# Cutting the two last weight loads of a decode kernel into pieces for unequally late DMA engines

## The chip, the cores and the metric

The kernel runs on one core of one Trainium2 chip. The metric is device time in microseconds (us), the median of several executions. The six executions of the kernel before lie within 0.62 us of each other, and the whole argument is about one microsecond in 1267. So the clean evidence is in the traces; the times only have to agree with it.

## The reference, cut to what matters

One decode step: attention of 16 query heads over 8 cached K/V heads of 65,536 positions and 256 dimensions, then the output projection `wo`; a small MLP beside it is cut here.

```python
q = (x @ wq).reshape(B, Sq, 16, 256).transpose(0, 2, 1, 3)
k = jnp.repeat(k_cache, 2, axis=1)      # k_cache, v_cache: 1 x 8 x 65536 x 256, bf16
v = jnp.repeat(v_cache, 2, axis=1)
p = softmax(einsum("bhqd,bhkd->bhqk", q, k) * 256 ** -0.5)
o = einsum("bhqk,bhkd->bhqd", p, v)
a = o.transpose(0, 2, 1, 3).reshape(B, Sq, 4096) @ wo     # wo: 4096 x 448
# ... MLP branch b and gate g cut ...
return g * a + (1 - g) * b
```

Reading the two caches once is 537 MB of the 544.22 MB that the kernel reads, at 430 GB/s over its 1264.3 us, and that is the kernel's time.

## The kernel before: the parts that matter

One queue (SP) issues all large loads: 32 K loads and 32 V loads of 8 MB, with the `wo` rows of a head pair between them. The last V load is cut into pieces along the sequence, so that the work behind each piece can start early. The `wo` rows of the last two query heads come last of all.

```python
pieces = [(NFIRST, NLATE), (NLATE, 124), (124, NV)]      # 96:112, 112:124, 124:128
# ... sync engine, last K/V block ...
load(vbuf, A_v_cache, j, 0, NFIRST if last else NV, 0, sem_v)
if last:
    for (n0, n1), sem in zip(pieces, sem_vp):
        load(vbuf, A_v_cache, j, n0, n1, 0, sem)
# ... cut ...
eng.wait_ge(s_proj, H - 1)
for h in range(REP):                                     # REP = 2
    w = A_wo[(HQ - REP + h) * DH:(HQ - REP + h + 1) * DH, :]
    eng.dma_start(wo_sb[:, h, :], w.rearrange("(p j) n -> p (j n)", j=2)).then_inc(sem_wl[h], 16)
```

The tensor engine's end: the matmuls on the two last V pieces, then the vector engine's normalised `oTn`, then the projection.

```python
def tail():
    pe.wait_ge(s_cp, H)
    by_d(sps[:, 0, 0:2 * REP])
    late_values(NLATE, NV).then_inc(s_late, 1)           # waits for the V pieces 112:124 and 124:128
    spin(1)
    pe.wait_ge(s_oTn, H)
    for h in range(REP):
        pe.wait_ge(sem_wl[h], 16)
        ins = project([dj * REP + h for dj in range(2)], 2 * h)
    ins.then_inc(s_proj, 1)
```

The softmax here doesn't subtract the row's maximum and nothing guards it: scores larger than these inputs give would overflow.

## Time and profile before

| | before |
|---|---|
| time, median of 6 runs | 1266.58 us (1266.24 to 1266.86) |
| span of the profiled run | 1264.3 us |
| HBM read | 544.22 MB, 430 GB/s over the span |
| increments of the V piece of tiles 96 to 111 (two before the last), first to last of 16 engines | 1255.84 to 1257.83 us |
| increments of the last V piece (tiles 124 to 127) | 1258.40 to 1260.35 us |
| increments of the last `wo` load | 1259.60 to 1261.53 us |

The last three rows are from the trace's semaphore records. Each of these loads has 16 increments there, one for each of the 16 DMA engines when its share has landed (the last packet of all ends at 1261.08, the last increment stands at 1261.53), so first-to-last is how far the engines are apart: 2 us. Most of that dates from the start. Each of eight 16 KB packets on the profile's `q8 instruction` queue, begun from 18.42 to 68.31 us, held one engine for 1.01 to 1.14 us. In the K and V increments one engine is about 1 us late at 21 us, three at 32, five at 52 and eight from 71 us on, and as all engines stay loaded they are still late at the end. (The spread is 1.93 to 2.03 us in every K, V and `wo` load from 70 us on; the rest of it is there from the first load, 0.73 us among the other fifteen.) The prediction shows the lines of the profile. The page says that all engines are busy to the end (nine tenths or more in 39 of its 40 slices, eight in the last), so only the order and the sharing in the last microseconds can matter. In the timeline, the bracket behind an instruction tells how long its engine sat idle before it and what ended that.

### The profile page before, as it was taken

To read this page: it belongs to the slowest core of one execution; us is meant where nothing else is said; L and a number is where in the kernel's file an instruction comes from. 1 tells how busy PE (TensorE), PEld (TensorE's weight loads), DVE (VectorE), ACT (ScalarE), POOL (GpSimd) and SP (SyncE) were. 2 spreads that over 40 slices of the span, in tenths; PEclk is the share of its full clock that TensorE was granted. 3 is DMA by queue.
4 is the path that set the end of the run, shared out by engine and by line. 5 is a ranking of instruction groups with operands and counts; after the bars stand their busy time and mean duration, and the time that the engine had idled before them with its cause. 6 is when DMAs were issued, how large, how long until landed. Compare 5 with 4: busy or idle time off the path is not lost.

```text
span 1264.3 us, 38824 instructions
## 1 busy us (share of the span) xinstructions
PE 916.7 (73%) x17110; PEld 864.9 (68%) x17110; DVE 420.4 (33%) x755; ACT 536.7 (42%) x786; POOL 0.9 (0%) x7
## 2 busy tenths in 40 slices
PE   3866678766788667786676876768767578676698
PEld 2766668766677666686666876658766578666687
DVE  2433334433344333443222332223322233322233
ACT  1453345543355433454333553335533355433455
POOL 0000000000000000000000000000000000000000
PEclk9887889877888877988878887879878898878989
DMA  9999999999999999999999999999999999999998
GB/s 410 428 432 431 435 433 433 431 435 433 431 435 433 433 431 435 431 435 431 435 433 429 433 435 435 431 435 431 431 433 435 435 431 435 431 431 433 435 425 363
DMA packets 11629, 544.39 MB, mean 431 GB/s; under 512 B 1376, under 2 KB 1634, under 8 KB 2914
## 3 DMA queue, kind: packets, MB, share of 16 engines
q1 hardware_dynamic: 11528, 544.22, 99.7%
q8 instruction: 8, 0.13, 0.0%
q10 hardware_dynamic: 90, 0.01, 0.0%
q14 instruction: 3, 0.02, 0.0%
HBM read 544.22 MB, written 0.00 MB: 430 GB/s over the span
## 4 chain that ended last, share of the span: by engine, by line
DMA 71%; PE 28%; issue 1%; SPq 0%; DVE 0%; ACT 0%; ACTq 0%
DMA kring<-in_A_k_cache_dram 68%; PE kst L297 24%; PE sps L317 4%; DMA wo_sb<-in_A_wo_dram 2%; PE acc L352 0%; SPq L230 0%; SPq L264 0%; SPq L227 0%; SPq L225 0%; PE acc L341 0%; DVE out_g L625 0%; PE prj L399 0%; ACT pT L650 0%; ACTq L650 0%
## 5 line engine op out<-in xcount | busy, mean ns | idle before, releaser
L661 ACT ACTIVATE ktT<-kst 128x1024 bf16<-128x1024 bf16 x512 | 499.0, 1021 | 668.1 <-PE kst L297 667.5
L297 PE MATMUL kst<-ident,kring 128*128 128x128 f32 x4096 | 556.4, 297 | 306.1 <-DMA kring<-in_A_k_cache_dram 295.3
L297 PEld LDWEIGHTS kst<-ident,kring 128*128 128x128 f32 x4096 | 506.5, 154 | 316.0 <-issue 313.3
L563 DVE COPY ktT<-kst 128x1024 bf16<-128x1024 bf16 x512 | 354.1, 692 | 763.2 <-PE kst L297 739.4
L317 PEld LDWEIGHTS sps<-qcur,ktT 128*128 128x128 bf16 x8192 | 237.8, 96 | 4.2 <-issue 1.7
L317 PE MATMUL sps<-qcur,ktT 128*128 128x2 bf16 x8192 | 236.6, 163 | 1.5 <-issue 1.5
L352 PE MATMUL acc<-vbuf,pT 128*2 128x256 bf16 x4080 | 147.6, 315 | 2.2 <-issue 1.5
L352 PEld LDWEIGHTS acc<-vbuf,pT 128*2 128x2 bf16 x4080 | 109.3, 96 | 32.3 <-issue 2.0
L650 ACT ACTIVATE pT<-sps 128x32 f32 x256 | 51.8, 202 | 16.6 <-PE sps L317 16.6
L341 PE MATMUL acc<-pT,ones_sq 128*128 128x32 bf16 x256 | 11.7, 178 | 12.3 <-ACT pT L650 12.3
L341 PEld LDWEIGHTS acc<-pT,ones_sq 128*128 128x128 bf16 x256 | 8.6, 97 | 15.2 <-ACT pT L650 14.9
L568 DVE COPY accs<-acc 128x288 f32<-128x288 f32 x8 | 3.7, 458 | 40.1 <-PE acc L352 40.1
L667 ACT ACTIVATE z_b<-z_b 128x448 bf16<-128x448 bf16 x14 | 8.1, 577 | 20.4 <-DVE z_b L550 20.4
L388 PEld LDWEIGHTS acc<-sel,accs 128*64 128x64 f32 x112 | 10.8, 214 | 0.9
L388 PE MATMUL acc<-sel,accs 128*64 128x1 f32 x112 | 11.4, 260 | 0.0
L425 PE MATMUL acc<-vbuf 42*128 42x42 bf16 x1 | 0.2, 215 | 8.4 <-DMA b_b<-in_B_b_dram 8.4
L425 PEld LDWEIGHTS acc<-vbuf 42*128 42x128 bf16 x1 | 0.1, 99 | 8.5 <-DMA b_b<-in_B_b_dram 8.5
L399 PE MATMUL prj<-wo_sb,oTn 128*1 128x112 bf16 x128 | 3.6, 240 | 3.2 <-DVE oTn L591 2.8
L556 DVE TENSOR_TENSOR gu<-wtmp,z_b 128x448 bf16<-128x448 bf16 x14 | 5.5, 392 | 1.0
L544 DVE TENSOR_TENSOR z_b<-wtmp,u_b 128x448 bf16<-128x448 bf16 x14 | 5.5, 392 | 1.0
L542 DVE TENSOR_TENSOR wtmp<-u_b 128x448 bf16<-128x448 bf16 x14 | 5.5, 392 | 1.1
L548 DVE TENSOR_TENSOR z_b<-u_b,wtmp 128x448 bf16<-128x448 bf16 x14 | 5.5, 392 | 1.0
(85 smaller groups left out, 79.7 us busy)
## 6 DMA issues: line engine op xcount, KB each, us to landing
kring<-in_A_k_cache_dram SPq DMA_DIRECT2D x4, 4096.0 KB, 24.4
vbuf<-in_A_v_cache_dram SPq DMA_DIRECT2D x1, 6144.0 KB, 24.5
wo_sb<-in_A_wo_dram SPq DMA_DIRECT2D x7, 448.0 KB, 27.6
vbuf<-in_A_wq_dram SPq DMA_DIRECT2D x1, 3072.0 KB, 10.2
vbuf<-in_A_v_cache_dram SPq DMA_DIRECT2D x1, 1024.0 KB, 26.6
vbuf<-in_A_v_cache_dram SPq DMA_DIRECT2D x1, 768.0 KB, 27.7
vbuf<-in_A_wq_dram SPq DMA_DIRECT2D x1, 512.0 KB, 11.0
vbuf<-in_A_v_cache_dram SPq DMA_DIRECT2D x31, 30.0
```

What stands on the lines that cost most here:

```text
L297: ins = pe.transpose(kst[:, b, i * P:(i + 1) * P], kring_f[:, at + NT * (k % DC) + 4 * b + i, :], ident[:, :])
L317: ins = pe.matmul(sps[:, par, 2 * nt:2 * nt + 2], ktT[:, par, b, ntl * DH + dj:(ntl + 1) * DH:2], qcur[:, dj, :], start=(dj == 0), stop=(d ...
L341: pe.matmul(acc[:, DENC:SELC], ones_sq[:, :], pT[:, r, :], start=False, stop=(r == BODY - 1), skip_group_check=True)
L352: ins = pe.matmul(acc[o:o + REP, 0:DH], pT[:, r, 2 * nt:2 * nt + 2], vbuf[:, n, :], start=False, stop=False, skip_group_check=True)
L388: ins = pe.matmul(dst[hh * HP:(hh + 1) * HP, i:i + 1], accs[:, i:DH:2 * REP], sel[:, hh:hh + 1], start=False, stop=True, skip_group_check= ...
L542: vec.tensor_tensor(W, U, U, op=ALU.mult)
L544: vec.tensor_tensor(Z, W, U, op=ALU.mult)
L548: vec.tensor_tensor(Z, U, W, op=ALU.add)
L563: vec.tensor_copy(ktT[:, k % KTB, b, :], kst_b[:, b, :]).then_inc(sem_ev[b], 1)
L650: act.activation(pT[:, bass.ds(p0 + k % DC, 1), :].rearrange("p o n -> p (o n)"), sps[:, k % 2, 0:2 * NT], AF.Exp, scale=scale).then_inc(s ...
L661: act.activation(ktT[:, k % KTB, b, :], kst_b[:, b, :], AF.Copy).then_inc(sem_ev[b], 1)
L667: act.activation(z_b[:, :], z_b[:, :], AF.Tanh).then_inc(s_tanh, 1)
```

## The change

Intent: engines that are early should take more rows of the last two loads, late ones fewer. Whole, such a load is 128 rows, 8 on each engine (on the engine whose increments come first, the two loads' increments are 0.59 us apart, as long as 8 packets of 74 ns). It is now cut into pieces of 96, 25, 5 and 2 rows, meant for 16, 5, 5 and 2 engines. I supposed that the same few, early ones, take all the short pieces, and called them engines 0 to 4. If so, and if each piece is dealt out evenly, two engines get 6 + 5 + 1 + 1 = 13 rows per load, three get 12 and eleven get 6: an estimate.

```diff
+    wo_cuts = [(0, 96), (96, 121), (121, 126), (126, P)]
...
-                eng.dma_start(wo_sb[:, h, :], w.rearrange("(p j) n -> p (j n)", j=2)).then_inc(sem_wl[h], 16)
+                rows = w.rearrange("(p j) n -> p (j n)", j=2)
+                for p0, p1 in wo_cuts:
+                    eng.dma_start(wo_sb[p0:p1, h, :], rows[p0:p1, :]).then_inc(sem_wl[h], 16)
...
-                    pe.wait_ge(sem_wl[h], 16)
+                    pe.wait_ge(sem_wl[h], 16 * len(wo_cuts))
```

## The prediction

> **What bounds the kernel now.** I read the page first: its row of DMA engine use and the first line of the chain that ended last.
>
> ```profile
> DMA  9999999999999999999999999999999999999998
> DMA 71%; PE 28%; issue 1%; SPq 0%; DVE 0%; ACT 0%; ACTq 0%
> ```
>
> All 16 DMA engines are busy from end to end, with the K and V cache; the page gives 544.22 MB of HBM reads at 430 GB/s. The change moves none of these bytes. It touches only the two loads of the last head's wo rows, the last thing in the queue. So only the last few microseconds can change, and I read the end of the chain of waits next (start, duration, what).
>
> ```profile
> 1225.54 5.29 PE acc L352 x128
> 1233.37 28.16 DMA wo_sb<-in_A_wo_dram
> ```
>
> The last wo load, issued at 1233.37, stands 28.16 us behind K and V data in the queue and is the last link. The timeline shows what hangs on it (start, duration, engine, line, count, idle before and who ended it).
>
> ```profile
> 1259.77 0.98 PE L373 MATMUL sps<-pT,vbuf 128*128 128x2 bf16 x32
> 1260.79 0.16 DVE L579 TENSOR_TENSOR oTn<-sps,rden 128x4 bf16<-128x4 f32 x1 [1.15 <-PE sps L373]
> 1261.08 0.27 PE L399 MATMUL prj<-wo_sb,oTn 128*1 128x112 bf16 x8
> 1261.57 0.27 PE L399 MATMUL prj<-wo_sb,oTn 128*1 128x112 bf16 x8 [0.22 <-DMA wo_sb<-in_A_wo_dram]
> 1261.89 0.33 DVE L625 SCALAR_TENSOR_TENSOR out_g<-prj,bcast,run_g 128x112 bf16<-128x112 f32 x1 [0.94 <-PE prj L399]
> 1262.25 0.65 SPq L266 DMA_DIRECT2D out_dram<-out_g  x1
> ```
>
> The first eight projection matmuls wait for the vector engine's oTn, the second eight for the second wo load. Everything after them is serial. The idle time of 0.22 us understates what the wait holds back: eight of these matmuls of 0.21 us (the tile's view) take 0.27 us together, so their starts lie within 0.06 us, and with the weights there the second eight could start near 1261.15. At most 0.42 us of the kernel can go.
>
> Now the DMA engines, by stretches of the end (after the clock: mean share of the 16 engines, GB/s).
>
> ```profile
> 1259.00:1259.50 0.50, 0.32 (x3) 0.32 (x3) 0.33 (x3) 0.00 (x0) 0.00 (x0) 1.00 0.94 349
> 1259.50:1260.00 0.50, 0.50 (x12) 0.46 (x12) 0.14 (x1) 0.00 (x0) 0.00 (x0) 1.00 0.67 245
> 1260.00:1260.50 0.50, 0.50 (x26) 0.50 (x23) 0.00 (x0) 0.00 (x0) 0.00 (x0) 1.00 0.52 194
> 1260.50:1261.00 0.50, 0.49 (x11) 0.18 (x8) 0.16 (x1) 0.00 (x0) 0.00 (x0) 1.00 0.20 72
> 1261.00:1261.50 0.50, 0.27 (x8) 0.13 (x8) 0.00 (x0) 0.00 (x0) 0.00 (x0) 1.00 0.00 0
> ```
>
> The engines run dry one after the other, over nearly 2 us: half of them sit idle at 1260.25, and three are still at it at 1260.8. That is the imbalance which the change goes for. The shares sum to (0.94 + 0.67 + 0.52 + 0.20) x 0.5 = 1.17 us of work per engine after 1259.0, so a perfectly level end would come at 1260.17 instead of 1261.08 (the end of the last packet in the trace's packet records).
>
> The trace's semaphore records, which no view prints, give every engine's increment. For the second wo load they land from 1259.60 to 1261.53: five by 1260.14, three from 1260.30 to 1260.39, five from 1260.84 to 1261.11, three from 1261.37 to 1261.53. The same 2.0 us of spread stands at every K and V load from 70 us on. Where it comes from, the queues of the stretch from 11 to 75 us show.
>
> ```profile
> q8 instruction: 8, 0.13, 0.8%
> q14 instruction: 2, 0.02, 0.1%
> ```
>
> Eight packets of 16 KB, one each on a different engine, each 1.01 to 1.14 us long. Linking packets end to end, I find that these eight engines are exactly the eight late ones: they lost a microsecond once and, all engines being equally loaded ever after, never made it up.
>
> [...]
>
> **The change part by part.** *Issue.* Six more DMAs on the SP queue at 0.43 us (the tile's view: 0.42 to 0.43 each) are 2.6 us more, ending near 1236.4. The data is wanted some 22 us later; all hidden. Six more increments on an early engine at 9 ns each are 0.05 us where there is slack.
>
> *Rows.* Before, every engine moves 8 rows of 1792 B per load, 16 in all. [...] A row costs 1.18 us / 16 = 0.0735 us (on the fastest engine the last two wo loads' increments and the V piece's before them land at 1258.40, 1259.01, 1259.60: 0.6 us per 8 rows). A late engine saves 4 rows, **0.29 us**: the last increment moves from 1261.53 to 1261.23. [...]
>
> *Path.* The first eight matmuls stay at 1261.08, set by V and oTn (the first wo load, at 1260.95 before, comes earlier still). The second eight start 0.04 us after 1261.23, at 1261.27 instead of 1261.57. Epilogue and output DMA move up with them. Sum: **-0.29 us**, or 0.023%.
>
> **The rivals.** *First, shared ports.* [...] The change would be -0.05 to +0.3 us. [...] Against it: some foreign rows come after V is through[...]. *Second, the wrong engines.* If engines 0 to 4 were late ones, they would carry 10 rows more: +0.73 us. [...] *Third, hidden anyway.* If the oTn path were the limit, nothing would move; the 0.42 us above says it isn't. *Fourth, code layout.* [...] one 8 KB packet costs 0.32 us on one engine (seen at 1235.94). It could go either way.
>
> **Range and chances.** I give the clean gain of -0.29 some 45%, shared ports at a mean of +0.1 us 45%, the other two 10% at about +0.2: -0.13 + 0.045 + 0.02 = about -0.07. I round the time to **1266.6 us**. The three runs before lie 0.31 us apart, which is as much as the effect. Adding -0.3 to +0.3 of effect and as much again of noise and placement gives **1266.0 to 1267.1**. Two per cent is 25 us, more than the whole tail, so the chances are 0.005 faster, 0.99 same, 0.005 slower.
>
> **What would show it.** Right: all the K and V landings unchanged until 1258; the second group of projection matmuls starts near 1261.27; the engines' use between 1258.5 and 1260 is higher and it drops sharply near 1260.8. Shared ports: the wo packets on the early engines take longer than 0.074 us each, V packets longer than before, the multiply of 1260.79 comes later. Wrong engines: three to five engines work alone well after 1261. The forecast of the time would be wrong by more than its range only if the new kernel's executions ran at another clock or placement, or if a short DMA costs far more on an engine than its rows.

The forecast's sum was -0.29 us for the clean gain (a late engine saves 2 of its 8 rows in each of two loads), -0.07 us with the rivals weighed in, so 1266.6 us. By the estimate the engines with the short pieces would not become the last: 26 rows for two loads, 26 x 0.0735 + 0.05 after an early engine's V increment at 1258.47, give 1260.43 us, and 24 rows after 1259.23 give 1261.04, both before 1261.23. (26 rows instead of 16 are the second rival's 10 rows more.) That early engines would be the ones to get them was not shown. "Foreign" rows are those that an engine writes into partitions which, as I supposed, a 128-row load gives to another engine. "Port" is my word for whatever would then be shared; no run shows one.

## The result, and the profile after

The changed kernel takes **1267.26 us** (median of 6 runs, 1266.95 to 1267.74), against 1266.58 before. The ratio is 1.0006, with a 95% interval of 0.9993 to 1.0018. Ratios are the mean time of one kernel's fast runs over that of the other's fast runs of the same rounds, so not quite the ratio of the medians. The two sets of runs do not overlap, though: it is some 0.7 us slower, and outside the range predicted.

In the chain that ended last, the last load is another one.

```profile
1232.02 29.68 DMA vbuf<-in_A_v_cache_dram
```

Before, the last `wo` load stood there; now it is the last V piece, which the change did not touch. The timeline of the end (start, duration, engine, line, operation, count, idle and what ended it):

```profile
1260.79 0.76 PE L379 MATMUL sps<-pT,vbuf 128*128 128x2 bf16 x24 [0.66 <-DMA vbuf<-in_A_v_cache_dram]
1261.74 0.35 PE L379 MATMUL sps<-pT,vbuf 128*128 128x2 bf16 x8 [0.20 <-DMA vbuf<-in_A_v_cache_dram]
1262.13 0.16 DVE L585 TENSOR_TENSOR oTn<-sps,rden 128x4 bf16<-128x4 f32 x1 [2.17 <-PE sps L379]
1262.35 0.50 PE L405 MATMUL prj<-wo_sb,oTn 128*1 128x112 bf16 x16
1262.90 0.33 DVE L631 SCALAR_TENSOR_TENSOR out_g<-prj,bcast,run_g 128x112 bf16<-128x112 f32 x1 [0.60 <-PE prj L405]
```

The late matmuls, one unbroken group from 1259.77 before, start at 1260.79 and stop once more, both times for V, whose last increment comes at 1261.69. `oTn` comes at 1262.13 instead of 1260.79. The sixteen projection matmuls then run in one group. The last increment of `wo` lands at 1262.49, when the first of them have started. So both have become later, V by 1.34 us and `wo` by 0.96. The stretches of the end (columns from the clock on: granted clock, DMA share, GB/s):

```profile
1259.00:1259.50 0.50, 0.00 (x0) 0.00 (x1) 0.45 (x1) 0.00 (x0) 0.00 (x0) 1.00 1.03 248
1259.50:1260.00 0.50, 0.50 (x4) 0.50 (x4) 0.35 (x2) 0.00 (x0) 0.00 (x0) 1.00 0.88 203
1260.00:1260.50 0.50, 0.13 (x2) 0.04 (x1) 0.00 (x0) 0.00 (x0) 0.00 (x0) 1.00 0.79 213
1260.50:1261.00 0.50, 0.21 (x8) 0.22 (x9) 0.00 (x0) 0.00 (x0) 0.00 (x0) 1.00 0.71 146
1261.00:1261.50 0.50, 0.50 (x22) 0.45 (x18) 0.00 (x0) 0.00 (x0) 0.00 (x0) 1.00 0.48 140
1261.50:1262.00 0.50, 0.30 (x11) 0.27 (x9) 0.00 (x0) 0.00 (x0) 0.00 (x0) 1.00 0.20 72
```

Read the last two columns together. From 1259.0 to 1259.5, engines with a busy share of 0.94 moved 349 GB/s before; now, with 1.03 (a packet is counted whole where it starts), they move 248. The engines are fuller, as intended, and deliver less: each packet takes longer. The trace's packet records say by how much, as means over the tail: V packets of 8192 B 313 ns before and 314 after, of 6144 B 238 and 252, of 2048 B 85 and 110 (at most 178), `wo` packets of 1792 B 78 and 109.

Two delays have to be told apart. The piece of tiles 96 to 111 is complete 0.32 us later than before, at 1258.15, before any `wo` packet can have disturbed it: its last packet ends at 1257.70 (an increment follows some 0.45 us later), the first `wo` packet starts at 1257.96. From there to the last V increment it is 3.54 us, against 2.52 before. I call this distance the **V lag**, and the distance to the last `wo` increment the **wo lag** (4.34 us, against 3.69). They take out the lateness that a run brings with it.

### The profile page after: what moved, and what is told of

Read it like the earlier page. It is cut to its first block, busy times and chain, and to the rows that moved or that the text cites. A ratio compares the mean times of both kernels' runs of the same rounds, so it can differ in the third digit from the quotient of the medians.

```text
span 1265.3 us, 38830 instructions
## 1 busy us (share of the span) xinstructions
PE 916.9 (72%) x17110; PEld 866.5 (68%) x17110; DVE 420.5 (33%) x755; ACT 537.2 (42%) x786; POOL 0.9 (0%) x7
## 4 chain that ended last, share of the span: by engine, by line
DMA 70%; PE 28%; issue 1%; SPq 0%; DVE 0%; ACT 0%; ACTq 0%
DMA kring<-in_A_k_cache_dram 68%; PE kst L303 24%; PE sps L323 4%; DMA vbuf<-in_A_v_cache_dram 2%; PE acc L358 0%; SPq L234 0%; PE prj L405 0%; SPq L229 0%; SPq L231 0%; PE acc L347 0%; PE sps L379 0%; DVE out_g L631 0%; PE kst L339 0%; ACT pT L656 0%; ACTq L656 0%
## 5 line engine op out<-in xcount | busy, mean ns | idle before, releaser
L358 PE MATMUL acc<-vbuf,pT 128*2 128x256 bf16 x4080 | 143.7, 309 | 2.4 <-issue 1.7
L560 DVE TENSOR_SCALAR z_b<-z_b 128x448 bf16<-128x448 bf16 x14 | 3.9, 277 | 5.5 <-ACT z_b L673 5.5
```

The costliest lines, as they stand in the source:

```text
L358: ins = pe.matmul(acc[o:o + REP, 0:DH], pT[:, r, 2 * nt:2 * nt + 2], vbuf[:, n, :], start=False, stop=False, skip_group_check=True)
```

## The experiments

Theory, **ports**: an engine that writes partitions which a 128-row load gives to another engine slows that engine down. (Which partitions a load gives to which engine is supposed; the runs below test what the supposition implies.) Rivals: **short DMAs** (more, shorter loads on few engines cost more wherever they write, or the added order of HBM reads does), **engine speed** (there is nothing to share, the row count per engine decides), and **chance** (the longer program or the run shifts the engines). V lag and wo lag come from the semaphore records of each run's one trace; times are medians. The four kernels in which, by the theory, nothing crosses (before, e5, e6, e8) have V lags within 0.04 us of each other; the two traces of the changed kernel differ by 0.12.

| run | time, us (before, same rounds) | V lag, us | wo lag, us |
|---|---|---|---|
| before | 1266.58 | 2.52 | 3.69 |
| changed | 1267.26 (1266.58) | 3.54 | 4.34 |
| e1_low_rows | 1267.21 (1266.60) | 3.42 | 4.47 |
| e2_halves | 1267.33 (1266.60) | 4.17 | 5.00 |
| e3_aside | 1267.60 (1266.60) | 3.40 | 4.42 |
| e5_columns | 1266.59 (1266.61) | 2.56 | 3.76 |
| e6_own | 1267.50 (1266.61) | 2.54 | 4.73 |
| e7_foreign | 1268.84 (1266.61) | 3.52 | 5.92 |
| e8_levelled | 1270.14 (1266.61) | 2.55 | 4.67 |
| e9_only96 | 1267.00 (1266.59) | 3.40 | 4.09 |
| e10_short_aside | 1267.29 (1266.59) | 2.91 | 4.08 |
| e12_again (one run) | 1267.14 (1266.59) | 3.42 | 4.53 |

### e1_low_rows: the short pieces at the other end

```diff
-    wo_cuts = [(0, 96), (96, 121), (121, 126), (126, P)]
+    wo_cuts = [(32, P), (0, 25), (25, 30), (30, 32)]
```

> The changed kernel with the short pieces at partitions 0 to 31 instead of 96 to 127: the same DMAs of 96, 25, 5 and 2 rows[...], results right. Ports[...]: [...] the last V piece lands 0.5 to 1.0 us earlier than in the changed kernel, the time is 1266.3 to 1266.8. Short DMAs (a piece on few engines costs more wherever it writes): as the changed kernel, 1267.0 to 1267.6.

The time is that of the changed kernel, and the V lag is 3.42 us. (By the clock the last V piece does land 0.62 us earlier than in the changed kernel, as expected for ports, but tiles 96 to 111 land 0.50 us earlier too: chance, as e12 shows.) As I had put it, this spoke for short DMAs and against ports. But there was a hole: I had taken it for granted that the 96-row piece itself keeps each engine to its own partitions.

### e2_halves: two pieces of 64 rows, nothing short, nothing unequal

```diff
-    wo_cuts = [(0, 96), (96, 121), (121, 126), (126, P)]
+    wo_cuts = [(0, 64), (64, P)]
```

> Each of the two last wo loads in two DMAs of 64 rows. Every engine keeps its 8 rows per load and every DMA runs on all 16 engines, but rows 64 to 127 are written by early engines too. Ports: V packets get longer as in the changed kernel, the last V piece lands 0.3 to 1.0 us later than before, time 1266.9 to 1267.6. Short DMAs or unequal shares of rows: nothing of that is here, so the time is that of before within 0.2 us.

The V lag is the largest of all with an unchanged amount of data, 4.17 us, though its pieces are equal and none is short (the same cut in bulk, e4, kept all the engines busy, with a share of 1.02). Short or unequal pieces are not needed for the loss. The time alone (1266.95 to 1268.30) would show little; the profiled run was the slowest.

### e3_aside: the short pieces into a spare tile at partitions 0 to 31

```diff
-                    eng.dma_start(wo_sb[p0:p1, h, :], rows[p0:p1, :]).then_inc(sem_wl[h], 16)
+                    to = wo_sb[p0:p1, h, :] if p0 < 96 else wo_aside[p0 - 96:p1 - 96, h, :]
+                    eng.dma_start(to, rows[p0:p1, :]).then_inc(sem_wl[h], 16)
```

> The changed kernel, but the short pieces (same source rows, [...]same count) land in a spare tile at partitions 0 to 31; the result is wrong on purpose. Ports: V packets keep their lengths of before (2048 B near 85 ns), the last V piece lands as before, the second wo load 0.3 us earlier, time 0.0 to 0.4 us below before. Short DMAs: as the changed kernel, 0.7 us above before.

Wrong on purpose (it was still within the test's tolerance). A miss like e1: V lag 3.40 us, V packets of 2048 B at 112 ns, time 1.0 us above before. Moving the short pieces away does not give V back. So what is common to e1, e2, e3 and the change is left: a load of 64 or 96 rows.

### e4_big_halves: the same cut where it can be weighed

```diff
+                if j == 16:
+                    for (p0, p1), sem in zip([(0, 64), (64, P)], (sem_v, sem_vh)):
+                        eng.dma_start(vbuf[p0:p1, :, :].rearrange("p n d -> p (n d)"),
+                                      src(A_v_cache, j)[p0:p1, :]).then_inc(sem, 16)
... else the whole load as before; the tensor engine's wait for the second half cut ...
```

> The kernel before with one V load of 8 MB in mid-kernel (the 17th of 32) cut into DMAs of partitions 0 to 63 and 64 to 127, each on all 16 engines. Ports: [...] its 4 MB take 19.4 us instead of 9.7; the kernel is about 19 us longer, near 1286, with half the GB/s in that stretch. An engine's own speed as the limit: no change, within 0.5 us of before.

1288.71 us in one run, 22.1 us more. The stretch from 680 to 690 us, of the kernel before and then of this one (last three columns: clock, DMA share, GB/s):

```profile
680.00:690.00 10.00, 5.21 (x128) 3.65 (x120) 0.00 (x0) 0.00 (x0) 0.00 (x0) 0.83 1.01 439
```

```profile
680.00:690.00 10.00, 2.06 (x69) 1.96 (x67) 0.69 (x1) 1.93 (x4) 0.00 (x0) 0.72 1.02 210
```

All engines are as busy as ever (1.02, against 1.01), at less than half the rate, for about 40 us. That is 8.39 MB at 210 GB/s, where whole loads move at 433; by the bytes alone it costs 20.6 us. Engine speed as the only limit is out: all engines have packets in hand, and are held back. Whether a 64-row load also reads HBM in a worse order, this run can't tell from where it writes. So in this profile a busy engine is one that has a packet in hand: a share of 1.02 stands beside 210 GB/s here and one of 1.01 beside 439 before.

### e5_columns: split without leaving 128 rows

```diff
+                for j in range(2):
+                    eng.dma_start(wo_sb[:, h, j * DM:(j + 1) * DM], rows[:, j * DM:(j + 1) * DM]).then_inc(sem_wl[h], 16)
... the wait raised from 16 to 32 ...
```

> Each of the two last wo loads in two DMAs that halve the columns, so that every DMA keeps its 128 rows[...]. Ports (what costs is an engine that writes partitions which a 128-row load gives to another engine): the last V piece lands 2.5 us after the last packets of the piece two before it, as before, and the time is that of before within 0.2 us. Splitting as such (more and shorter DMAs beside the V loads): V lands later by half of what the changed kernel showed or more, time 0.3 us or more above before.

Twice the DMAs and half the packet size, and nothing happens: 1266.59 us, V lag 2.56. Splitting as such is free here. The second from 1258.5 to 1259.5 us, before and in e5:

```profile
1258.50:1259.50 1.00, 0.44 (x9) 0.32 (x3) 0.67 (x3) 0.00 (x0) 0.00 (x0) 1.00 0.95 355
```

```profile
1258.50:1259.50 1.00, 0.43 (x9) 0.32 (x3) 0.67 (x3) 0.00 (x0) 0.00 (x0) 1.00 0.97 332
```

### e6_own and e7_foreign: one difference, the partition written

Eight added loads of 8 rows, into partitions 0 to 63 in e6 and 64 to 127 in e7: `to` is `p0` in e6 and `p0 + 64` in e7. The packet records of e6 show eight engines running them. I supposed that in e6 each of these writes the partitions that it has in a 128-row load.

```diff
+            aside = A_wo[(HQ - REP) * DH:(HQ - REP + 1) * DH, :].rearrange("(p j) n -> p (j n)", j=2)
+            for p0 in (0, 1, 2, 3, 32, 33, 34, 35):
+                to = p0 + 0          # e7: p0 + 64
+                eng.dma_start(wo_aside[to:to + 29:4, :], aside[p0:p0 + 29:4, :]).then_inc(sem_aside, 16)
... the two wo loads as before; a wait for sem_aside before the output cut ...
```

> The kernel before with eight added loads of 8 rows of 1792 B into a spare tile, just ahead of the last wo loads[...] Ports: V lands as before; the early engines use up 0.6 us of their slack; time as before within 0.2 us. Short DMAs or the added reads of HBM: the same rise as in e7_foreign, 0.4 us or more.

> As e6_own, [...]same source rows, same count, but 64 partitions further up (64 to 127)[...]. Ports: the last V piece and the last wo load land 0.5 to 1.0 us later than in e6_own, time 0.4 to 1.0 us above before. Short DMAs or HBM reads: no difference from e6_own.

The same stretch, e6_own and then e7_foreign:

```profile
1258.50:1259.50 1.00, 0.44 (x14) 0.16 (x2) 0.58 (x2) 0.00 (x0) 0.00 (x0) 1.00 0.99 364
```

```profile
1258.50:1259.50 1.00, 0.48 (x4) 0.48 (x4) 0.81 (x3) 0.00 (x0) 0.00 (x0) 1.00 0.99 226
```

With equal share, 364 against 226 GB/s. Source rows, sizes, count and order are the same; in the programs only the destination differs. (That e6 keeps each engine to its own partitions is supposed; its V lag fits.) The V lag is 2.54 in e6, as before, and 3.52 in e7; V packets of 2048 B average 85 and 117 ns; the times, 1266.98 to 1267.81 and 1268.06 to 1269.08, do not overlap. This settles it for these loads: what costs V is the destination. Short DMAs by themselves leave V alone. And it costs more than the rows themselves: 64 rows on eight engines are 8 x 0.0735 = 0.59 us for each (an estimate, with the price of a row from the trace before), and V lost 0.99.

The time of e6 was a miss: 0.9 us above before, where none was expected. Its wo lag shows where it is, 4.73 us. In the packet records two of the eight engines that ran the 8-row loads (known by their pattern of one row, one increment) were among the late ones in the V loads, the fourth-last and the last. They carried the added rows, and their last packets ended at 1261.59 and 1262.20, those of all others by 1260.90. So the eight engines that take such loads are not simply the early eight. Nor did the rows cost only their 0.59 us: the wo lag grew by 1.04. On the last engine the increments of the added loads come evenly, at 1261.67, 1261.86, 1262.07 and 1262.27, before those of the two `wo` loads at 1262.48 and 1262.73; the last ones of e7 and e8 are 0.2 us apart too. That is nearly three times the 0.0735 us of a row. Why is not shown.

### e8_levelled: the same aim without crossing

Partitions 0 to 63 get six units of 896 B and the others two; one 128-row load, then eight loads of 8 rows into partitions 0 to 63, with the destinations of e6.

```diff
+            eng.dma_start(wo_full[:, :, :], wl[:, 0:P, :].rearrange("h p n -> p h n")).then_inc(sem_wl[0], 16)
+            half = wl[:, P:DH, :].rearrange("h (p j) n -> p h (j n)", j=2)
+            for p0 in (0, 1, 2, 3, 32, 33, 34, 35):
+                eng.dma_start(wo_half[p0:p0 + 29:4, :, :], half[p0:p0 + 29:4, :, :]).then_inc(sem_wl[1], 16)
... tiles and views of the new layout, late matmuls and projection in three parts of 128, 64 and 64 dimensions ...
```

> The aim of the change by another way: the last two heads' wo rows are laid out so that partitions 0 to 63 hold six units of 896 B and partitions 64 to 127 two; one 128-row load takes the two units, eight loads of 8 rows take the other four[...] Ports: V lands as before, the last wo increment comes about 0.4 us earlier than before, time 0.1 to 0.4 us below before (half as many more late matmuls take a little back). Short DMAs: as the changed kernel or worse, 0.5 us or more above before.

Right for V (lag 2.55 us), and a failure as a kernel: 3.5 us slower. The tensor engine took it. The late matmuls of this kernel in its timeline (before: 32 of them in 0.98 us):

```profile
1259.73 4.75 PE L379 MATMUL sps<-pT,vbuf 128*128 128x2 bf16 x48
```

48 matmuls, two thirds of them with 64 columns of weights between ones with 128, need 0.10 us each instead of 0.03; which of the two, the smaller shape or the change of shape, was not tested. And the last `wo` increment came no earlier either, at 1262.41, after increments 0.2 us apart, as in e6.

### e9_only96 and e10_short_aside: the shares of the two kinds of piece

```diff
-    wo_cuts = [(0, 96), (96, 121), (121, 126), (126, P)]
+    wo_cuts = [(0, 96)]                                   # e9: wrong on purpose
```

```diff
+                eng.dma_start(wo_sb[:, h, :], rows).then_inc(sem_wl[h], 16)            # e10
+                for p0, p1 in [(96, 121), (121, 126), (126, P)]:
+                    eng.dma_start(wo_aside[p0:p1, h, :], rows[p0:p1, :]).then_inc(sem_aside, 16)
... a wait for sem_aside before the output cut ...
```

> The changed kernel with only its 96-row pieces: rows 96 to 127 of the two last wo loads are not loaded (wrong result on purpose). A quarter of the bytes is gone and there is no short piece. Ports, with the 96-row piece itself dealt across them: the last V piece still lands 0.4 to 1.0 us later after the piece two before it than the 2.5 us of before. Ports, with a 96-row piece that keeps to its own: V as before, and the time 0.1 to 0.3 us below before.

> The kernel before, its two wo loads whole, and behind each of them the change's three short pieces as added loads into partitions 96 to 127 of a spare tile. Ports: V lands 0.3 to 0.6 us later than before by the short pieces alone. If the 96-row pieces are the whole of the loss: V as before.

The stretch from 1258.5 us in e9:

```profile
1258.50:1259.50 1.00, 0.43 (x7) 0.37 (x4) 0.72 (x3) 0.00 (x0) 0.00 (x0) 1.00 0.95 226
```

With a quarter of the bytes left out and no short piece, V still lags by 3.40 us: the 96-row pieces alone cost it 0.88 us. The short pieces alone (e10) cost 0.39, inside what the port theory expected; there they are added bytes behind whole loads, so not quite the change's own. Together (the change) they cost 0.90 to 1.02, less than the sum. e1 and e3, with the short pieces elsewhere, cost 0.90 and 0.88 as well, so beside the 96-row pieces the short ones add nothing clear of the 0.12 us between traces.

### e11_big_cut: the change's own cut, in mid-kernel

```diff
-                    for (p0, p1), sem in zip([(0, 64), (64, P)], (sem_v, sem_vh)):
+                    for (p0, p1), sem in zip([(0, 96), (96, 121), (121, 126), (126, P)], (sem_v, sem_vh, sem_vh, sem_vh)):
... the tensor engine's wait raised from 16 to 48 ...
```

> The kernel before with one V load of 8 MB in mid-kernel (the 17th of 32) cut as the change cuts the wo loads: 96, 25, 5 and 2 rows. Ports: clearly longer than before, by 5 to 20 us, with the GB/s down in that stretch though no DMA engine is idle. An engine's own speed as the limit: [...] those engines run 10 to 12 us behind the others and K and V wait for them, but the GB/s in that stretch stays near 430 until the others run out of work.

1318.89 us in one run: 52.3 us more, far beyond the 5 to 20 expected. ("Those engines" are the ones with the short pieces, 12 or 13 rows instead of 8 by the estimate above, at the 2.42 us of a 64 KB packet before.) Two stretches (same columns as above):

```profile
680.00:690.00 10.00, 1.95 (x68) 1.84 (x66) 0.66 (x1) 1.82 (x4) 0.00 (x0) 0.71 1.09 222
...
710.00:720.00 10.00, 0.00 (x0) 0.00 (x0) 0.00 (x0) 0.00 (x0) 0.00 (x0) 0.50 0.60 120
```

The first lies in the 96-row piece. In the packet records its 64 KB packets take 4.5 to 5.1 us on all 16 engines, against 2.42 in whole loads: the piece moves at half rate for its 30 us. The half rate lasts some 20 us longer, with the short pieces and the next loads in the queues. In the second stretch all 16 engines still have a packet in hand, most of them of 7 to 9 us (few start there, hence the share of 0.60); only from 728 to 735 us do five engines work alone.

### e12_again: is the rest chance?

The changed kernel, unaltered, for a second trace.

> The changed kernel once more, for a second trace. Ports: the last V piece lands 3.4 to 3.7 us after the piece two before it (3.54 in its first trace, 2.52 before). The lateness of the K and V landings ahead of it, 0.3 us more than before in the first trace, differs from trace to trace if it is chance, and is the same if the longer program causes it.

V lag 3.42 us, as in the first trace within 0.12. The piece of tiles 96 to 111 was complete at 1257.68, 0.15 us earlier than before instead of 0.32 later. Over all traces of the tail that time lies between 1257.65 and 1258.18, whatever the kernel. So the 0.32 us of the first trace is chance, and the lag is the change's.

## Why the prediction was wrong

- **What bounds it, and the size of the prize**: right. The last V piece and the last `wo` load set the end, and nothing up to 1258.15 us moved by more than two traces of one kernel differ (0.47 us).
- **Issue** (hidden): right. All eight DMAs were issued by 1238.6 us, more than 19 us before their first packet (one issue alone took 3.60 us and delayed nothing).
- **Rows**: the numbers of engines fit (28 increments per load), the price of a row did not. "A row costs 0.0735 us" was read from loads of 128 rows and used for pieces of other shapes. (1.18 / 16 is 0.0738, and the increments quoted beside it give 0.075; that changes no sum by more than 0.04 us.) In the changed kernel a `wo` packet averaged 109 ns instead of 78, and the last `wo` increment came 0.64 us later after tiles 96 to 111, not 0.29 us earlier.
- **Path**: "The first eight matmuls stay at 1261.08, set by V and oTn" is the step that failed. V landed 1.02 us later after tiles 96 to 111 (0.90 in the second trace), and the projection started at 1262.35. The saving was to come from the second eight matmuls alone; in fact the loss of V held back all sixteen.
- **First rival, shared ports**: right in its signs, mis-sized, and not shown as a mechanism. All three of its signs came: `wo` packets of 109 ns (mean of all engines), V packets of 2048 B at 110 instead of 85, the multiply at 1262.13. That the destination costs V is shown by e6 against e7 (V lag 2.54 against 3.52 us), for added loads of 8 rows; that one engine there writes another's partitions is my reading. That the 96-row pieces lose by the same is what fits e2, e4, e9 and e11, but where each of their rows goes was not seen, and a worse order of HBM reads in such loads was not tested apart. My 0.29 us for it counted only the short pieces, which measured 0.39 alone. The 96-row pieces were taken as harmless and measured 0.88 alone. The rival's "-0.05 to +0.3 us" became 0.7 us in the medians, and the 45% I gave it was too little: with the caches' bulk loads all of 128 rows, nothing in the trace spoke for harmless partial ones.
- **Second rival, the wrong engines**: my evidence against it was weaker than I thought. In e6 two of the eight engines that took the 8-row loads were late. For the engines of the short pieces in the changed kernel itself, the lengthened packets could not be linked with certainty, so whether one of them was late there stays open. The sign named for it does not decide: some three engines work alone at the end (share 0.20 from 1261.5 to 1262.0), but so they did before (0.20 from 1260.5 to 1261.0).
- **Third rival** (hidden) did not occur. **Fourth, code layout** (the longer program shifts the engines): the shift between traces is there, 0.5 us in all, and two traces of the one changed kernel differ by as much (e12), so it is chance. Nor was the clock another one (0.841 to 0.844 in all runs of the changed kernel).

Also open: how the rows of a 96-row load are dealt to the engines. That it runs at half rate throughout is measured (210 to 222 GB/s in e11, against 433); why exactly half is not. No run here beats the kernel before: e5 equals it, and giving more work to eight of the engines (e6, e8) fails: in e6 two of those eight were late.

## What to carry to other kernels

Before you rebalance transfers between DMA engines, check whether the destination partitions stay what they were, and read the GB/s beside the engines' busy share: in e6 and e7 the share was 0.99 both times, and moving the destination by 64 partitions took 364 GB/s down to 226. When a load has to be cut, try first to split it along the free dimension, with all 128 partitions kept: that was free here (e5, 1266.59 us against 1266.61, V lag 2.56). And test a new transfer shape once in bulk, where it cost 22 us (e4) and 52 us (e11), before you read tenths in a tail.
